# Bases of the decay powers by broadcast transfers, the idle products in one stretch, and the bias as three bf16 products

## The chip, the cores and the metric

The kernel runs on one core of a Trainium2 chip. The metric is the device time of one execution in microseconds; the median of several runs counts. Beside it stands a profiled execution with its trace. The core has five engines that run side by side and wait for each other by semaphores: TensorE (PE, with its weight loads PEld), VectorE (DVE), ScalarE (ACT), GpSimd (POOL) and SyncE (SP), which here only issues transfers. ACT issues a few transfers of its own at the start.

## The reference, cut to what matters

Lightning attention with a decay per head, and a highway layer on its result. There are 4 batches, 8 heads, 768 positions and 64 channels; `lam` is one number per head, and all powers of it are wanted.

```python
Dmask = np.where(rel >= 0, lam[:, None, None] ** rel[None, :, :], 0.0)
lam_pow = lam[:, None, None] ** (pos[None, :, None] + 1)
...
    intra = np.einsum('bhic,bhjc->bhij', qb, kb) * Dmask[None]
    intra = np.einsum('bhij,bhjd->bhid', intra, vb)
    inter = np.einsum('bhid,bhde->bhie', qb * lam_pow[None], kv_state)
    out[:, :, sl] = intra + inter
    kv_state = lam_block[None, :, None, None] * kv_state + np.einsum('bhsd,bhse->bhde', kb_dec, vb)
...
H = np.maximum(x @ w_h, 0.0)
T = 1.0 / (1.0 + np.exp(-(x @ w_t + b_t)))
return (T * H + (1.0 - T) * x).astype(np.float32)
```

Here `x` is the attention's output as 3072 rows of 512, `w_h` and `w_t` are 512 by 512, and `b_t` is a row of 512. Everything is f32 outside; the products on PE are of bf16 numbers, summed in f32.

## The kernel before, in words

The sequence of each batch is cut into three stages of 256 positions, so there are 12 stages, numbered 0 to 11. The decay is put into the operands: q is multiplied by growing powers of lam (`cast_q`, L225 to L235, tile `qb`) and v by falling ones (`cast_v`, L237 to L240, tile `vs`), so that the scores need only a triangular mask. In a stage, k and q are transposed on PE (`trans`, L251, into `bktr` and `bqtr`), copied out of PSUM (`evac_k`, `evac_q`, whose copies go by the helper at L110 for ACT and L112 for DVE and POOL, tiles `kT` and `qT`), multiplied to scores (L279), masked on DVE (L336), and multiplied with v (L358). The state `kv` is summed in PSUM (L284), copied to `ss`, and multiplied with q (L352). The result is copied to `xT` and goes through the two 512 by 512 products of the layer (L388), a sigmoid on ACT, and DVE and POOL work, to the output.

The powers need `lam` on all 128 partitions in two layouts: all eight heads in each row, and for each row the two heads that it holds. Before the change `lam` is brought in as a tile `lam_r` of 4 by 2, and two f32 products (L156, L157) spread it: one with ones and a matrix `lam_d` made on DVE (L152), one with `pick`, a repeated identity (L150). ACT takes the logarithm of the result in PSUM (`ln`, L161), DVE multiplies it with the positions (L163, L168), and ACT takes the exponentials `pow_q8` (L166) and `pow_v` (L171). `cast_q` and `cast_v` of every stage wait for these.

PE does idle products on zeros meanwhile: four at L125, ahead of the two f32 products, and six at L159 behind them; later the plan has spins of the same kind (`spin`, L429).

The bias of the sigmoid is put on all partitions once: `bias` (L426) multiplies a row of ones with `b_r` in f32 into PSUM, DVE copies the result to `b_bc` (token BC), and `begin` (L391) copies `b_bc` into each PSUM tile of the sigmoid's product before that product is added.

The order of the work is written out by hand. What stands before L176 is issued in the order of the program; then come the tokens of PLAN (L17 to L68), one after the other, each issuing its instructions to its engine. Every engine works through its own list in that order. A token is a name, a stage, further indices, `@` and the engine, `=` and PSUM banks. The first ones are a spin (Z.1), the loads and casts of stage 0 (Lv, CV on POOL, Lq, CQ on POOL and DVE), PT, which loads ACT's second activation table, the transposes TQ and TK, their copies EQ and EK, then scores S, states U, the copy KE, masks M; `B=1` is the bias product, and I.0 (L352) follows it on PE. Transfers are issued by SP in the order of the plan, with the two small ones, `lam_r` (L116) and `b_r` (L118), by ACT ahead of everything.

Of the kernel before, what the change touches and what calls it, by code (L numbers as in the profile page):

```python
# [8 lines left out]
F32 = mybir.dt.float32  # L9
BF16 = mybir.dt.bfloat16  # L10
I32 = mybir.dt.int32
AF = mybir.ActivationFunctionType
ALU = mybir.AluOpType
# [1 line left out]


PLAN = """  # L17
Z.1=0 Lv.0.1 CV.0.1@POOL Lq.0.1 CQ.0.1@POOL PT@ACT Lq.0.0 CQ.0.0@DVE TQ.0.2=1 EQ.0.1@ACT Lk.0.0 CK.0.0@DVE TK.0.0=2
Lk.0.1 CK.0.1@POOL EQ.0.0@DVE TK.0.1=3 EK.0.0@ACT EK.0.1@ACT S.0.0=45 Lv.0.0 CV.0.0@DVE U.0.0 KE.0.0@ACT M.0.0.0@DVE
Lq.1.1 S.0.1=60 B=1 M.0.1.0@DVE M.0.1.1@DVE M.0.0.1@DVE BC@DVE I.0=23 U.0.1 KE.0.1@DVE Lq.1.0 CQ.1.2@POOL A.0.0 Lk.1.1  # L20
Lk.1.0 CK.1.2@ACT Lv.1.0 TQ.1.2=4 EQ.1.2@ACT A.0.1 TK.1.2=5 EK.1.2@ACT Z.3=0 D.0.0@ACT Lv.1.1 CV.1.2@DVE SS.1.1=61
# [52 lines left out]
def kernel(  # L74
# [12 lines left out]
    B, H, S, D = q.shape  # L87
    C = 128
    NST = S // (2 * C)
    NP = H // 2  # L90
    DM = H * D
# [6 lines left out]
    singles = ctx.enter_context(tc.tile_pool(name="singles", bufs=1))  # L98
    sb = ctx.enter_context(tc.tile_pool(name="sb", bufs=1))
    ps = ctx.enter_context(tc.tile_pool(name="ps", bufs=1, space=bass.MemoryType.PSUM))  # L100

    V, A, P, T = nc.vector, nc.scalar, nc.gpsimd, nc.tensor
# [5 lines left out]
    def copy(eng, dst, src):  # L108
        if eng == "ACT":
            A.activation(dst, src, AF.Copy)  # L110
        else:
            ENG[eng].tensor_copy(dst, src)  # L112


    lam_r = singles.tile([NP, 2], F32)
    A.dma_start(out=lam_r, in_=lam.rearrange("(h e) -> h e", e=2))  # L116
    b_r = singles.tile([1, DM], F32)
    A.dma_start(out=b_r, in_=moe_b_t.rearrange("(o f) -> o f", o=1))  # L118
    blank = singles.tile([128, 512], BF16)
    V.memset(blank, 0.0)  # L120
    id128 = singles.tile([128, 128], BF16)
    make_identity(nc, id128)
    cold = ps.tile([128, 512], F32, tag="b5", name="cold", bufs=1)
    for _ in range(4):
        T.matmul(cold, lhsT=blank[:, 0:128], rhs=blank, start=True, stop=True)  # L125
    tk_i = singles.tile([128, NST, J], I32)
    P.iota(tk_i, pattern=[[2 * C, NST], [1, J]], base=0, channel_multiplier=J)
# [13 lines left out]
    V.tensor_scalar(row_f, in0=row_i, scalar1=float(Q // NP), scalar2=None, op0=ALU.mult)  # L141
    tq_f = singles.tile([128, NST, Q], F32)
    V.tensor_scalar(tq_f, in0=tq_i, scalar1=row_f, scalar2=None, op0=ALU.add)
    id_f = singles.tile([NP, NP], F32)
    V.tensor_copy(id_f, id128[0:NP, 0:NP])
    A.preload_act_table_set("natural_log_exp_and_others")
    ones = singles.tile([NP, 128], F32)
    V.memset(ones, 1.0)
    pick = singles.tile([NP, 128 // NP, NP], F32)
    V.tensor_copy(pick, id_f[:, None, :].to_broadcast([NP, 128 // NP, NP]))  # L150
    lam_d = singles.tile([NP, NP, 2], F32)
    V.tensor_tensor(lam_d, in0=id_f[:, :, None].to_broadcast([NP, NP, 2]), in1=lam_r[:, None, :].to_broadcast([NP, NP, 2]), op=ALU.mult)  # L152
    kv = ps.tile([128, NP, 128], F32, tag="kv", name="kv", bufs=1)
    V.memset(kv, 0.0)
    lam_ps = ps.tile([128, H + 2], F32, tag="b6", name="lam_ps", bufs=1)
    T.matmul(lam_ps[:, 0:H], lhsT=ones, rhs=lam_d.rearrange("k h e -> k (h e)"), start=True, stop=True, skip_group_check=True)  # L156
    T.matmul(lam_ps[:, H:H + 2], lhsT=pick.rearrange("k p h -> k (p h)"), rhs=lam_r, start=False, stop=True, skip_group_check=True)  # L157
    for _ in range(6):
        T.matmul(cold, lhsT=blank[:, 0:128], rhs=blank, start=True, stop=True)  # L159
    ln = singles.tile([128, H + 2], F32)  # L160
    A.activation(ln, lam_ps, AF.Ln)  # L161
    p_lq = singles.tile([128, NST, 2, Q], F32)
    V.tensor_tensor(p_lq, in0=ln[:, None, H:H + 2, None].to_broadcast([128, NST, 2, Q]),  # L163
                    in1=tq_f[:, :, None, :].to_broadcast([128, NST, 2, Q]), op=ALU.mult)
# [4 lines left out]
                    in1=tk_f[:, :, None, :].to_broadcast([128, NST, H, J]), op=ALU.mult)  # L169
    pow_v = singles.tile([128, NST, H, J], F32)  # L170
    A.activation(pow_v, p_ln, AF.Exp, scale=-1.0)  # L171
    b_bc = singles.tile([128, DM], F32)
    w_f = [singles.tile([128, KC, DM], F32, name=f"w_f{i}") for i in range(2)]
    w_b = [singles.tile([128, KC, DM], BF16, name=f"w_b{i}") for i in range(2)]

# [11 lines left out]
    def bank(key, i, shape, dtype=F32):  # L187
        if key not in made:
            made[key] = ps.tile(shape, dtype, tag=f"b{i}", name=f"b{key[0]}", bufs=1)
        return made[key]  # L190

    def get(*key):
        return made[key]
# [178 lines left out]
    def cols(p):  # L372
        if p > 2:
            return slice(128 * p - 384, 128 * p - 256)
        return slice(0, DM) if p == 2 else slice(256 * p, 256 * p + 256)
# [15 lines left out]
    def begin(n, b, p, eng, bk):  # L391
        z = cols(p)
        copy(eng, bank(("t", n, b, p), bk[0], [C, z.stop - z.start]), b_bc[:, z])
# [23 lines left out]
    def store(n, parts):  # L417
        i = 2 * n * C
        for p in parts:
            nc.sync.dma_start(out=out[i:i + 2 * C].rearrange("(b p) f -> p b f", p=C)[p], in_=get("o_sb", n)[p])  # L420

    def store_part(n, b, p):
        i = (2 * n + b) * C
        nc.sync.dma_start(out=out[i:i + C, cols(p)], in_=get("o_sb", n)[:, b, cols(p)])

    def bias(bk):  # L426
        T.matmul(bank(("bias",), bk[0], [128, DM]), lhsT=ones[0:1], rhs=b_r, start=True, stop=True)  # L427

    def spin(r, bk, idle=[0]):  # L429
        idle[0] += 1  # L430
        t = bank(("spin", idle[0]), bk[0], [128, 512])
        for _ in range(r):
            T.matmul(t, lhsT=id128, rhs=blank, start=True, stop=True)  # L433
# [13 lines left out]
        "TX": lambda a, e, bk: rows(*a, bk), "F": lambda a, e, bk: block(*a, bk), "H": lambda a, e, bk: relu(*a),  # L447
        "G": lambda a, e, bk: sigm(*a), "X": lambda a, e, bk: rest(*a), "Y": lambda a, e, bk: total(*a, e),
        "ST": lambda a, e, bk: store(*a, (slice(0, 119), slice(119, C)) if e else (slice(0, C),)) if len(a) == 1 else store_part(*a),
        "B": lambda a, e, bk: bias(bk), "BC": lambda a, e, bk: copy(e, b_bc, get("bias")), "BP": lambda a, e, bk: begin(*a, e, bk), "Z": lambda a, e, bk: spin(*a, bk),  # L450
        "PT": lambda a, e, bk: A.preload_act_table(AF.Sigmoid),
    }
    in_place = set()
# [3 lines left out]
    for token in PLAN.split():  # L457
        token, _, bk = token.partition("=")
        token, _, eng = token.partition("@")
# [32 lines left out]
```

## Time and profile before

| what | us |
|---|---|
| median of 3 runs (105.47, 106.03, 106.33) | 106.03 |
| profiled execution | 105.67 |
| its span, first to last instruction | 103.6 |
| PE busy in it | 95.2 |
| DVE, ACT, POOL busy | 85.9, 70.1, 71.6 |
| DMA, mean rate over the span | 266 GB/s |

Starts are counted from the first instruction. A profiled execution is longer than its span by what lies before and after it, here 2.07 us. In the busy rows one digit is a fortieth of the span, in tenths; PEclk is the clock that PE was granted. In the chain of waits every piece is what the next one waited for, or what stood before it on the same engine. The timeline gives start, duration, engine, line, and the tile written and the tiles read; in square brackets stands the idle time before and what ended it.

### The profile page before, as it was taken

To read this page: it belongs to the slowest core of one execution; us is meant where nothing else is said; L and a number is where in the kernel's file an instruction comes from. 1 tells how busy PE (TensorE), PEld (TensorE's weight loads), DVE (VectorE), ACT (ScalarE), POOL (GpSimd) and SP (SyncE) were. 2 spreads that over 40 slices of the span, in tenths; PEclk is the share of its full clock that TensorE was granted. 3 is DMA by queue.
4 is the path that set the end of the run, shared out by engine and by line. 5 is a ranking of instruction groups with operands and counts; after the bars stand their busy time and mean duration, and the time that the engine had idled before them with its cause. 6 is when DMAs were issued, how large, how long until landed. Compare 5 with 4: busy or idle time off the path is not lost.

```text
span 103.6 us, 3953 instructions
## 1 busy us (share of the span) xinstructions
PE 95.2 (92%) x1667; PEld 61.0 (59%) x1687; DVE 85.9 (83%) x148; ACT 70.1 (68%) x113; POOL 71.6 (69%) x64
## 2 busy tenths in 40 slices
PE   5976998999999999999999999999999999999940
PEld 1524475576547666577767665668666767555630
DVE  4475863779599979999999999998997988899980
ACT  3446327959738879786599879997684786475410
POOL 6192702655979999999995059799899974255450
PEclk9999557999999999999999999999999999999997
DMA  1999999999999999999999999998310491047564
GB/s 35 311 302 341 293 362 355 384 328 331 285 326 311 307 309 320 292 342 272 286 317 325 376 360 344 367 313 278 136 75 0 168 384 69 0 166 274 216 224 139
DMA packets 33483, 27.52 MB, mean 266 GB/s; under 512 B 1465, under 2 KB 26425, under 8 KB 33466
## 3 DMA queue, kind: packets, MB, share of 16 engines
q1 hardware_dynamic: 33456, 27.27, 84.3%
q8 instruction: 13, 0.21, 0.8%
q14 instruction: 4, 0.03, 0.2%
q10 hardware_dynamic: 10, 0.00, 0.0%
HBM read 20.97 MB, written 6.29 MB: 263 GB/s over the span
## 4 chain that ended last, share of the span: by engine, by line
PE 86%; DVE 4%; POOL 2%; ACT 2%; issue 2%; DVEq 0%; POOLq 0%
PE bh L388 20%; PE bt L388 19%; PE bs L279 9%; PE bo L358 7%; PE bqtr L251 6%; PE bx L382 6%; PE bktr L251 5%; PE bo L352 5%; PE kv L284 3%; PE bbias L427 2%; PE cold L125 2%; POOL qb L233 1%; POOL vs L239 1%; ACT kT L110 1%; PE bspin L433 1%
## 5 line engine op out<-in xcount | busy, mean ns | idle before, releaser
L336 DVE TENSOR_TENSOR m<-bs,tri 128x512 bf16<-128x512 f32 x48 | 31.0, 683 | 2.5 <-PE bs L279 2.0
L415 POOL TENSOR_TENSOR ob<-y,w 128x512 f32<-128x512 bf16 (+1 forms) x20 | 22.2, 1119 | 14.9 <-DVE y L402 9.6
L388 PEld LDWEIGHTS <-xT 128*128 128x128 bf16 x208 | 18.0, 98 | 16.0 <-issue 0.2
L388 PE MATMUL bh<-w_b,xT 128*128 128x512 bf16 (+2 forms) x95 | 23.2, 361 | 0.5
L388 PE MATMUL bt<-w_b,xT 128*128 128x512 bf16 (+2 forms) x94 | 23.2, 361 | 0.5 <-issue 0.2
L239 POOL TENSOR_TENSOR vs<-vf,pow_v 128x1024 bf16<-128x1024 f32 (+1 forms) x11 | 21.0, 1912 | 3.4 <-ACT pow_v L171 2.2
L397 ACT ACTIVATE g<-bt 128x512 f32<-128x512 f32 (+2 forms) x26 | 14.5, 565 | 10.2 <-PE bt L388 7.3
L233 POOL TENSOR_TENSOR qb<-qf,pow_q 128x1024 bf16<-128x1024 f32 (+1 forms) x10 | 18.6, 1858 | 1.7 <-DMA qf<-in_q_dram 1.7
L408 DVE SCALAR_TENSOR_TENSOR w<-g,bx 128x512 bf16<-128x512 f32 (+2 forms) x26 | 16.0, 639 | 1.3 <-ACT g L397 1.0
L110 ACT ACTIVATE qT<-bqtr 128x1024 bf16<-128x1024 bf16 (+1 forms) x12 | 11.9, 989 | 5.6 <-PE bqtr L251 5.6
L110 ACT ACTIVATE xT<-bo 128x512 bf16<-128x512 f32 x22 | 12.6, 597 | 4.1 <-PE bo L358 4.0
L279 PE MATMUL bs<-qT,kT 64*64 64x128 bf16 x384 | 14.7, 222 | 0.6 <-ACT kT L110 0.5
L402 DVE SCALAR_TENSOR_TENSOR y<-bh,g 128x512 bf16<-128x512 f32 (+1 forms) x20 | 13.1, 665 | 1.5 <-PE bh L388 1.3
L279 PEld LDWEIGHTS <-kT 64*64 64x64 bf16 x384 | 11.3, 108 | 5.0 <-issue 2.5
L110 ACT ACTIVATE ss<-kv 128x512 bf16<-128x512 f32 x15 | 9.0, 597 | 4.1 <-PE bs L279 3.3
L110 ACT ACTIVATE bt<-b_bc 128x512 f32<-128x512 f32 (+1 forms) x18 | 10.4, 586 | 0.3
L284 PE MATMUL kv<-vs,kb 64*64 64x64 bf16 x320 | 9.8, 201 | 0.3 <-DVE vs L239 0.2
L358 PE MATMUL bo<-m,vs 64*64 64x128 bf16 x384 | 8.5, 226 | 0.0
L251 PE MATMUL bktr<-id,kb 128*128 128x128 bf16 x96 | 7.9, 226 | 0.7 <-POOL kb L112 0.7
L284 PEld LDWEIGHTS <-kb 64*64 64x64 bf16 x320 | 8.0, 111 | 0.8 <-issue 0.8
L251 PE MATMUL bqtr<-id,qb 128*128 128x128 bf16 x96 | 7.8, 227 | 0.6 <-POOL qb L233 0.6
L358 PEld LDWEIGHTS <-vs 64*64 64x64 bf16 x384 | 6.3, 110 | 2.9 <-issue 2.3
(63 smaller groups left out, 111.2 us busy)
## 6 DMA issues: line engine op xcount, KB each, us to landing
vf<-in_v_dram SPq DMA_DIRECT2D x24, 256.0 KB, 5.9
qf<-in_q_dram SPq DMA_DIRECT2D x24, 256.0 KB, 5.5
kf<-in_k_dram SPq DMA_DIRECT2D x24, 256.0 KB, 5.4
out_dram<-ob SPq DMA_DIRECT2D x11, 512.0 KB, 3.9
w_f<-in_moe_w_t_dram SPq DMA_DIRECT2D x2, 512.0 KB, 5.9
w_f<-in_moe_w_h_dram SPq DMA_DIRECT2D x2, 512.0 KB, 8.3
out_dram<-ob SPq DMA_DIRECT2D x1, 256.0 KB
out_dram<-ob SPq DMA_DIRECT2D x2, 64.0 KB, 1.8
```

Source lines behind the costliest of these rows:

```text
L110: A.activation(dst, src, AF.Copy)
L233: ENG[eng].tensor_tensor(new(("qb", n), [128, Q, 2, D])[:, :, es].rearrange("p j e d -> p e j d"), in0=get("qf", n)[:, es].rearrange("p e ...
L239: ENG[eng].tensor_tensor(new(("vs", n), [128, H, J, D])[:, heads(p)], in0=get("vf", n)[:, heads(p)].rearrange("p h (j d) -> p h j d", j=J) ...
L251: T.transpose(t[:, i], turned(x, n, c), id128)
L279: T.matmul(get("s", n, e, hp // 2)[half(b), hp % 2, j, :], lhsT=get("kT", n)[half(e), hp, j, half(b)], rhs=get("qT", n)[half(e), hp, b * C ...
L284: T.matmul(kv[half(e), hp, half(e)], lhsT=get("kb", n)[half(b), j, 2 * hp + e, :], rhs=get("vs", n)[half(b), 2 * hp + e, j, :], start=firs ...
L336: V.tensor_tensor(new(("m", n, e, u), [128, 2, J, C]), in0=get("s", n, e, u), in1=tri[:, None].to_broadcast([128, 2, J, C]), op=ALU.mult)
L358: T.matmul(get("o", n, b)[half(e), hp, :], lhsT=get("vs", n)[half(b), 2 * hp + e, j, :], rhs=get("m", n, e, hp // 2)[half(b), hp % 2, j, : ...
L388: T.matmul(t, lhsT=get("xT", n)[:, j, b * C:(b + 1) * C], rhs=w_b[w][:, j, z], start=(j == 0 and not w), stop=(j == KC - 1), skip_group_ch ...
L397: A.activation(new(("g", n, b), [C, DM], F32)[:, z], get("t", n, b, p), AF.Sigmoid)
L408: V.scalar_tensor_tensor(new(("w", n, b), [C, DM])[:, z], in0=get("g", n, b)[:, z], scalar=1.0, in1=x.rearrange("p j f -> p (j f)")[:, z], ...
L415: ENG[eng].tensor_tensor(o, in0=y, in1=get("w", n, b)[:, z], op=ALU.subtract)
```

## The change

The bases come as two transfers onto 128 partitions, into one tile `lam_b`, in place of the two f32 products and what made their operands. All fourteen idle products stand ahead; the six behind the f32 products are gone with these. The bias is split into three bf16 terms that sum to it: b_s[0] is the bias rounded, b_d the rest, b_s[1] that rounded, b_s[2] what is then left. Four tokens BS.0 to BS.3 do this at the very head of the plan, on ACT, DVE, ACT and DVE; the bias product becomes three bf16 products added in PSUM.

```diff
 PLAN = """
-Z.1=0 Lv.0.1 CV.0.1@POOL Lq.0.1 CQ.0.1@POOL PT@ACT Lq.0.0 CQ.0.0@DVE TQ.0.2=1 ...
+BS.0@ACT BS.1 BS.2@ACT BS.3 Z.1=0 Lv.0.1 CV.0.1@POOL Lq.0.1 CQ.0.1@POOL PT@ACT Lq.0.0 CQ.0.0@DVE TQ.0.2=1 ...
...
-    lam_r = singles.tile([NP, 2], F32)
-    A.dma_start(out=lam_r, in_=lam.rearrange("(h e) -> h e", e=2))
+    lam_b = singles.tile([128, H + 2], F32)
+    A.dma_start(out=lam_b[:, 0:H], in_=lam.rearrange("(o h) -> o h", o=1).to_broadcast([128, H]))
+    A.dma_start(out=lam_b[:, H:H + 2], in_=lam.rearrange("(o h e) -> o h e", o=1, e=2).to_broadcast([128 // NP, NP, 2]))
     b_r = singles.tile([1, DM], F32)
     A.dma_start(out=b_r, in_=moe_b_t.rearrange("(o f) -> o f", o=1))
...
-    for _ in range(4):
+    for _ in range(14):
         T.matmul(cold, lhsT=blank[:, 0:128], rhs=blank, start=True, stop=True)
...
-    id_f = singles.tile([NP, NP], F32)
-    V.tensor_copy(id_f, id128[0:NP, 0:NP])
     A.preload_act_table_set("natural_log_exp_and_others")
-    ones = singles.tile([NP, 128], F32)
-    V.memset(ones, 1.0)
-    pick = singles.tile([NP, 128 // NP, NP], F32)
-    V.tensor_copy(pick, id_f[:, None, :].to_broadcast([NP, 128 // NP, NP]))
-    lam_d = singles.tile([NP, NP, 2], F32)
-    V.tensor_tensor(lam_d, in0=id_f[:, :, None].to_broadcast([NP, NP, 2]), in1=lam_r[:, None, :].to_broadcast([NP, NP, 2]), op=ALU.mult)
     kv = ps.tile([128, NP, 128], F32, tag="kv", name="kv", bufs=1)
     V.memset(kv, 0.0)
-    lam_ps = ps.tile([128, H + 2], F32, tag="b6", name="lam_ps", bufs=1)
-    T.matmul(lam_ps[:, 0:H], lhsT=ones, rhs=lam_d.rearrange("k h e -> k (h e)"), start=True, stop=True, skip_group_check=True)
-    T.matmul(lam_ps[:, H:H + 2], lhsT=pick.rearrange("k p h -> k (p h)"), rhs=lam_r, start=False, stop=True, skip_group_check=True)
-    for _ in range(6):
-        T.matmul(cold, lhsT=blank[:, 0:128], rhs=blank, start=True, stop=True)
     ln = singles.tile([128, H + 2], F32)
-    A.activation(ln, lam_ps, AF.Ln)
+    A.activation(ln, lam_b, AF.Ln)
...
+    b_s = singles.tile([1, 3, DM], BF16)
+    b_d = singles.tile([1, DM], F32)
+    one_b = singles.tile([1, 128], BF16)
+    P.memset(one_b, 1.0)
...
+    def split(i, eng):
+        if i == 0:
+            copy(eng, b_s[:, 0], b_r)
+        elif i == 1:
+            V.tensor_tensor(b_d, in0=b_r, in1=b_s[:, 0], op=ALU.subtract)
+        elif i == 2:
+            copy(eng, b_s[:, 1], b_d)
+        else:
+            V.tensor_tensor(b_s[:, 2], in0=b_d, in1=b_s[:, 1], op=ALU.subtract)
+
     def bias(bk):
-        T.matmul(bank(("bias",), bk[0], [128, DM]), lhsT=ones[0:1], rhs=b_r, start=True, stop=True)
+        t = bank(("bias",), bk[0], [128, DM])
+        for i in range(3):
+            T.matmul(t, lhsT=one_b, rhs=b_s[:, i], start=(i == 0), stop=(i == 2))
```

On the engines' lists this stands as follows. ACT issues three transfers (`lam_b` twice, then `b_r`), loads its first table, does ln and the two exponentials, then BS.0 and BS.2, then the second table load. DVE does the two products behind ln, then BS.1 and BS.3, then its half of `qb`. PE does fourteen idle products and the spin, then the transposes. SP's list is as before. POOL writes `one_b` ahead of its first `vs`.

## Prediction

> **What bounds the kernel now.** I read the busy slices first, then the chain of waits of the first 22 us in order of time, then the timeline of 0 to 14 us for what stands behind each step, then the stages for the clock and the DMA rings by stretch for when the small transfers land.
>
> ```profile
> PE   5976998999999999999999999999999999999940
> PEclk9999557999999999999999999999999999999997
> ```
>
> A digit is 2.6 us. (The first 9s of the clock are no measure: the idle products there step by 0.43 us, twice the 0.216 of full rate.) From about 17 us to 100 us PE is the bound: no wait of PE longer than 0.5 us is left there. So what PE gains or loses before 17 us should reach the end nearly whole. The change touches only what lies before 13.4 us.
>
> ```profile
> 4.12 0.19 ACT ln L161
> 4.57 0.24 ACT pow_q L166
> 4.81 0.14 ACT pow_v L171
> 5.09 1.04 POOL vs L239
> 6.13 1.46 POOL qb L233
> 7.63 0.63 PE bqtr L251 x8
> 8.29 0.60 ACT qT L110
> 8.92 0.69 DVE qT L112
> 9.61 0.61 DVE vs L239
> 10.26 0.53 PE kv L284 x12
> 10.90 0.43 PE bs L279 x14
> 11.32 2.00 PE bbias L427 x2
> 13.32 0.54 PE bo L352 x4
> ```
>
> These are the two places that count. The powers come from ln at 4.12, through POOL's products, to the first transposes (bqtr) at 7.63; and the f32 bias product holds PE for 2.00 us, from 11.32 to 13.32. What it holds back, bo of L352, needs ss, which ACT had at 11.53 (10.93 and 0.60), so all of the bias is on the path.
>
> ```profile
> 1.25 1.89 PE L125 MATMUL cold<-blank 128*128 128x512 bf16 x4 [1.25 <-DVE blank L120]
> 2.86 0.15 DVE L152 TENSOR_TENSOR lam_d<-id_f,lam_r 4x8 f32<-4x8 f32 x1
> 4.97 1.28 ACT L451 ACT_TABLE_LOAD   x1
> 5.88 0.80 DVE L233 TENSOR_TENSOR qb<-qf,pow_q 128x512 bf16<-128x512 f32 x1 [1.23 <-DMA qf<-in_q_dram]
> 8.29 0.60 ACT L110 ACTIVATE qT<-bqtr 128x512 bf16<-128x512 bf16 x1 [2.04 <-PE bqtr L251]
> ```
>
> Here DVE makes its half of qb at 5.88 to 6.68, 0.95 us before the transposes; ACT has nothing to do from 6.25 (4.97 and 1.28) to 8.29. That is all the slack into which the four new steps (BS.0 to BS.3) are put.
>
> **The change part by part.** The profiled execution took 105.67 us, of which 103.6 are the span; the median of the three runs is 106.03, so 0.36 is added to what comes out for the profiled one.
>
> *Bias.* Removed: 2.00 us of PE. Added: three bf16 products of 512 columns. The granted clock is 0.5 from 10.2 to 17.0 us. A product of that size at the low rate is the idle one: six of them step by 0.43 (the weight loads before them start at 4.41, 4.84, 5.27, 5.69, 6.12). Three cost 1.28, so the path gets 0.72 shorter. At the full clock (four bh products in 0.86 us, 0.216 each) they would cost 0.65; that end belongs to a rival.
>
> *Bases of the powers.* Removed from PE: the two f32 products (0.52 and 0.43 on the chain); from DVE: id_f, ones, pick and lam_d (0.15, 0.17, 0.37, 0.15), all ahead of ln. ln then waits for two transfers of 128 rows (32 and 8 bytes a row), ACT's first and second issue, with b_r third. Issues cost ACT 0.55 for lam_r and 0.23 for b_r, and SP 0.64 for 128 rows of qf (1.27 for two). With 0.55 for each of the new ones, from 0.80, the first table load starts near 2.2 instead of 1.64 and ends near 3.5 (1.28): ln is not sooner than that. When does the second transfer land? Nothing in this trace is it, so from both sides. The low end is lam_r: issued at 0.80, used at 2.86 without a wait, thus 2.06 at most; from 1.38 that gives 3.45. The high end is qf, also 128 rows: 3.5 from issue to landing in the first 2 us, so 4.9. The nearest is b_r, which was issued at that very place, 1.38:
>
> ```profile
> q10 hardware_dynamic: 8, 0.00, 0.2%
> ...
> q10 hardware_dynamic: 1, 0.00, 1.3%
> ...
> q10 hardware_dynamic: 1, 0.00, 0.1%
> ```
>
> The ring of ACT moved lam_r's eight packets before 2.0 us, one packet of b_r between 2.6 and 3.0, and its last between 3.0 and 3.5. SP's ring moved 417 packets between 2 and 3 us, so 128 rows want 0.3 us more: I take 3.8. ln then starts at 3.8 instead of 4.12, and pow_v, 0.83 after the start of ln as before (4.12 to 4.95), is done at 4.63.
>
> *The split of the bias, BS.0 to BS.3.* It stands ahead of the whole plan, so on ACT it is queued before the second table load and the copy of qT, and on DVE before qb. It alternates between the two: ACT, DVE, ACT, DVE, each waiting for the other. They work on one row of 512, but the time of the rows goes by the length of a row: ACT's 512 copies take 0.60 (xT; 0.64 from SBUF, w_b), DVE's products of 512 take 0.68 alone (vs) and 0.80 beside POOL's qb, which is running here; I take 0.74. With 0.03 for each hand-over (ln ends 4.30, p_lq starts 4.33): 0.60 + 0.03 + 0.74 + 0.03 + 0.60 + 0.03 + 0.74 = 2.77, from 4.63 to 7.40. Only then does DVE come to qb, which its data would have let it do at 5.88: 0.68, to 8.08, and 0.05 to PE. The transposes start at 8.13 instead of 7.63: **0.50 later**. POOL, which was last, is done with its half by about 7.3 (vs and qb start 0.32 sooner) and no longer matters. The table load follows BS.2 (6.63) and ends at 7.91, before qT at 8.8: hidden, with 0.9 to spare. From bqtr to kv every step of the chain hands on to the next with 0.02 to 0.05 us, so 0.50 reaches kv; the kf that held up kb on POOL (landed at 8.47) comes in that shade.
>
> *Idle products.* Fourteen at 0.43 are 6.0 us: 1.25 to 7.25 instead of 6.75, the spin after them to 7.7. PE waits for qb until 8.13, so they cost nothing; if qb came at 7.6 the spin would just reach it.
>
> *Rest.* one_b on POOL: its 64x256 selections end at 2.85 and it waits for pow_v until 5.09, so free. kv's memset on DVE moves up by 0.9 us into idle time. SP's list is the same.
>
> **Sum:** 0.50 later at kv, 0.72 saved at the bias: 0.22 sooner at bo. Downstream follow work that ACT and PE do back to back (transposes of the second stage, kT at 17.31), and its data wait for PE and not the reverse: qb of that stage is on hand at 12.69 and used at 14.85. So 105.67 - 0.22 = 105.45 for the profiled execution, 106.03 - 0.22 = **105.8 us** for the median. Bounds: with ln at 3.5 and the short durations (0.60, 0.68) qb is ready 0.08 later than before, in all 0.64 sooner, 105.4; with 4.9 and the long ones (0.64, 0.80) bqtr starts 1.92 later, in all 1.2 later, 107.2.
>
> **Rivals.**
>
> *The small transfers come late (slower).* Same place, ln's wait. At the landing of qf, 4.9, with my middle durations: pow_v 5.73, BS.3 8.50, bqtr 9.23, 1.60 later; less 0.72: 0.88, **106.9 us**. It decides from a landing at 4.02 on, where the loss equals 0.72. For it: b_r, with a single row, did not move until 2.6 although it was issued by 1.61. Against: the rows here carry 40 bytes, not 2 KB. The Trainium skill, page "DMA: Bandwidth & Descriptors", section "Issuing engines are not separate DMA queues", says that transfers issued by ACT and by SP run on the same 16 engines and interleave; by that rule the late landing and 106.9 are what to expect, by lam_r's row 105.4, and b_r's packets are on the rule's side.
>
> *The clock rises one stretch sooner (faster by more).* PE was busy 3.34 of 3.40 us between 10.2 and 13.6 and the clock stayed at 0.5; after 13.6 to 17.0 it rose. The first stretch differs by 2 us of one-row f32 products. If bf16 products count there and the f32 ones did not, the rise comes at 13.6. The work of 13.86 to 17.29 on the chain then goes at nearly double rate (8 transposes in 0.45 instead of 0.97, 32 bo in 0.57 against 16 in about that): some 1.5 us less, with 0.22 a total of 1.7, **104.3 us**. Against it: the new products have one row too. The Trainium skill, page "TensorE: Matmul & The Clock Gate", section "What's actually happening", has the full clock follow a busy window of 3.4 us that runs free of the kernel; the steps at 10.2 and 17.0 are two such windows apart, which agrees, but what counts as busy this trace can't say.
>
> *The loads are pushed back.* 256 rows more at 417 a us are 0.6 us for every load behind them. kb on POOL is then done at 9.7 instead of 9.08, and the scores start some 0.6 later instead of 0.5: in all 0.1 sooner, **105.9 us**, no change.
>
> **How the numbers follow.** Forecast 0.60, late transfers 0.22, clock 0.12, loads 0.06. A difference of 1% (1.06 us) is about what a measurement of this kernel tells from none. The forecast and the pushed loads lie within it; the clock is beyond it, faster, nearly always; late transfers reach over 107.1 only with the long durations, about half the time: faster 0.12, same 0.76, slower 0.12. The range 104.9 to 107.0 leaves out most of the clock and the top of the late transfers. The likeliest's own range is 105.3 to 106.4.
>
> **What would show it.** Right: DVE goes from BS.3 straight to qb near 7.4, without a wait for qf; bqtr near 8.1; the bias about 1.3 us on PE; bo of L352 (now L344) near 13.1. Wrong: ln after 4.2 (late transfers); a PEclk back at 9 by 14 us (clock); a DVE qb still at 5.9, which would mean that the order of the queue is not what holds it; a PE wait for DMA or POOL between 17 and 30 us that takes back what was won.

## The result, and the profile after

The changed kernel takes 111.5 us (median of 4 runs, 110.13 to 111.85), against 105.75 for the kernel before beside it. The ratio is 1.050, with a 95% interval of 1.037 to 1.064: slower by 5%, where 105.8 us and no change had been forecast. The profiled execution took 110.13 us with a span of 108.2, 4.6 more than the span before. One thing is needed to read single times: executions of one and the same kernel differ by 2 us and more (13 of the kernel before in one batch: 104.1 to 107.5), so every ratio compares the faster executions of the two kernels.

The busy slices of the page after, 2.7 us to a digit:

```profile
PE   5930679989999999999999999999999999999950
PEclk9999655599999999999999999999999999999997
```

PE now has a hole in the third to fifth slice, and the clock's 5s come later. From the ninth slice on the rows look as before: all of the loss is made in the first 22 us. The chain of waits there, in order of time (start, duration, what):

```profile
1.28 5.64 DMA lam_b<-in_lam_dram
...
7.01 0.22 ACT ln L149
7.24 0.02 issue
7.26 0.22 DVE p_lq L151
7.48 0.02 issue
7.50 0.24 ACT pow_q L154
7.74 0.13 ACT pow_v L159
7.88 0.53 ACT b_s L110
8.40 0.02 issue
8.43 1.19 DVE b_d L422
9.61 0.02 issue
9.63 0.64 ACT b_s L110
10.27 0.02 issue
10.30 0.75 DVE b_s L426
11.05 0.61 DVE qb L225
11.66 0.14 issue
11.80 1.02 PE bqtr L243 x8
...
15.02 0.53 PE kv L276 x9
...
16.08 1.39 PE bbias L431 x3
17.47 0.54 PE bo L344 x4
```

Read it against the chain before, station by station:

| from, to | before | after | more |
|---|---|---|---|
| start to the end of pow_v | 4.95 | 7.88 | 2.93 |
| to the first transposes (bqtr 7.63, 11.80) | 2.68 | 3.92 | 1.24 |
| to the bias (11.32, 16.08) | 3.69 | 4.28 | 0.59 |
| the bias itself | 2.00 | 1.39 | -0.61 |
| sum, at bo (13.32, 17.47) | | | 4.15 |
| bo to the end of the span | 90.3 | 90.7 | 0.4 |

The first row is the largest: a transfer of 128 rows of 8 bytes was issued at 1.28 and ln could not start before 7.01. The 0.59 of the third row are the transposes, now at half rate (1.02 instead of 0.63), and DVE's vs (0.81 instead of 0.61). The stages show two more things (columns: stretch and its length, then the busy time of PE, PEld, DVE, ACT and POOL, the granted clock, the DMA share and GB/s):

```profile
2.60:6.80 4.20, 3.70 (x13) 1.26 (x11) 0.44 (x1) 1.28 (x1) 0.46 (x2) 1.00 0.51 151
6.80:10.20 3.40, 0.00 (x0) 0.00 (x0) 1.50 (x3) 1.67 (x5) 2.18 (x2) 1.00 1.13 333
10.20:13.60 3.40, 1.80 (x16) 1.62 (x16) 1.82 (x4) 2.10 (x4) 3.35 (x3) 0.68 1.13 317
13.60:17.00 3.40, 2.68 (x52) 1.67 (x51) 3.40 (x6) 2.12 (x4) 0.82 (x1) 0.50 1.13 323
17.00:20.40 3.40, 3.40 (x62) 2.34 (x60) 2.85 (x4) 0.63 (x2) 1.38 (x2) 0.50 1.07 361
```

While the small rows go, the transfers move 151 GB/s, where they moved 296 before. PE, without work from about 6.3 to 11.8, then works at half rate up to about 21.7: some 10.2 us of it, where it was 6.8.

### The profile page after: what moved, and what is told of

The parts are those of the page before. It is cut to its first block, busy times and chain, and to the rows that moved or that the text cites. A ratio compares the mean times of both kernels' runs of the same rounds, so it can differ in the third digit from the quotient of the medians.

```text
span 108.2 us, 3958 instructions
## 1 busy us (share of the span) xinstructions
PE 95.1 (88%) x1668; PEld 61.3 (57%) x1688; DVE 86.9 (80%) x146; ACT 71.2 (66%) x115; POOL 74.9 (69%) x65
## 4 chain that ended last, share of the span: by engine, by line
PE 76%; DVE 9%; DMA 5%; ACT 3%; issue 3%; ACTq 0%; DVEq 0%
PE bh L380 19%; PE bt L380 18%; PE bs L271 8%; PE bo L350 7%; PE bqtr L243 6%; PE bktr L243 5%; DMA lam_b<-in_lam_dram 5%; PE bx L374 5%; PE bo L344 4%; PE kv L276 3%; DVE m L328 2%; PE bbias L431 1%; DVE b_d L422 1%; ACT b_s L110 1%; DVE vs L231 1%
## 5 line engine op out<-in xcount | busy, mean ns | idle before, releaser
L407 POOL TENSOR_TENSOR ob<-y,w 128x512 f32<-128x512 bf16 (+1 forms) x20 | 22.3, 1121 | 16.8 <-DVE y L394 11.8
L389 ACT ACTIVATE g<-bt 128x512 f32<-128x512 f32 (+2 forms) x26 | 14.5, 565 | 10.3 <-PE bt L380 7.0
L225 POOL TENSOR_TENSOR qb<-qf,pow_q 128x1024 bf16<-128x1024 f32 (+1 forms) x10 | 19.6, 1962 | 0.1
L243 PEld LDWEIGHTS <-qb 128*128 128x128 bf16 x96 | 6.4, 105 | 7.6 <-issue 6.0
```

The costliest lines, as they stand in the source:

```text
L225: ENG[eng].tensor_tensor(new(("qb", n), [128, Q, 2, D])[:, :, es].rearrange("p j e d -> p e j d"), in0=get("qf", n)[:, es].rearrange("p e ...
L243: T.transpose(t[:, i], turned(x, n, c), id128)
L389: A.activation(new(("g", n, b), [C, DM], F32)[:, z], get("t", n, b, p), AF.Sigmoid)
L407: ENG[eng].tensor_tensor(o, in0=y, in1=get("w", n, b)[:, z], op=ALU.subtract)
```

## The experiments

The theory after the result, A: the landing of the second small transfer delays ln by 2.9 us; the split, standing ahead of DVE's qb, adds 1.2; the bias gives 0.6 back. The rivals: B, the split costs most; and for the landing three causes, A1 small rows, A2 the same few bytes read by all rows, A3 any rows of ACT among SP's loads. A2 is called "one address" in the expectations. To be exact, the second transfer reads four pairs of numbers of lam, 32 bytes in all, each pair for 32 rows; the first reads these 32 bytes for each of its 128 rows. Later came C (DVE and POOL stop each other), with D (a late load) as its rival, and E (the clock), with F (PE waits for other engines and loads anyway). Times of one batch are compared with the kernel before in that batch; batches ran on different chips, so two changed kernels are compared by their ratios or their traces.

### Each half alone

Bases by transfers and the fourteen products, with the bias left in f32:

```diff
-BS.0@ACT BS.1 BS.2@ACT BS.3 Z.1=0
+Z.1=0
...
-            T.matmul(t, lhsT=one_b, rhs=b_s[:, i], start=(i == 0), stop=(i == 2))
+        T.matmul(bank(("bias",), bk[0], [128, DM]), lhsT=one_f, rhs=b_r, start=True, stop=True)
```

> Bases by the two transfers and the fourteen idle products, the bias still one f32 product and no split. Theory A (the landing of the second small transfer costs about 2.9 us at ln, the split the rest): ln near 7.0, bqtr 2.7 after the end of pow_v, so near 10.6, the bias 2.0 on PE; 109 us, 3 over before. Rival B (the alternating split at the head of the queues costs most): ln near 7.0 matters little, time within 1 us of before.

Measured: ln at 6.68, bqtr at 10.23, 110.54 us (four executions, 108.11 to 111.91) against 105.99. A stands, and B, which wanted the time within 1 us of before, does not; by the median 1.5 us more were lost than A had worked out. DVE's vs took 2.39 us here instead of 0.68, and the clock was at half until 24.2.

The other half, f32 bases with the split at the head of the plan and three bf16 products:

> Bases by f32 products as before, the bias split at the head of the plan and three bf16 products. Theory A: ln at 4.1 as before, bqtr 0.9 to 1.2 later than 7.63, the bias 0.6 shorter: 105.9 to 106.4 us, no change that 1% shows. Rival B: 109 us or more.

Measured: 108.6 us. ln at 4.12 and bqtr at 8.87, 1.24 later, as A has it; but the whole lost 2.6 by the median, where A had said 0.2 to 0.7. The four executions lie between 106.37 and 109.05, so the size is not settled. The profiled one took 109.05; in its trace bo, behind the bias, starts 2.1 us later than before and the end comes 3.7 later. The timeline between 10.3 and 13.2 us shows one thing beside the wait:

```profile
10.46 1.90 POOL L237 TENSOR_TENSOR qb<-qf,pow_q 128x1024 bf16<-128x1024 f32 x1 [0.93 <-DMA qf<-in_q_dram]
10.75 2.15 DVE L243 TENSOR_TENSOR vs<-vf,pow_v 128x512 bf16<-128x512 f32 x1
12.96 0.47 PE L288 MATMUL kv<-vs,kb 64*64 64x64 bf16 x10 [1.43 <-DVE vs L243]
```

Before, DVE's vs ran at 9.53, ahead of POOL's qb at 10.79, in 0.68 us. Pushed back by 1.2, it falls right behind the start of POOL's 1.9 us and ends 0.54 after POOL does. Theory C: the two do not share, one waits until the other's instruction is over. The same is seen in the changed kernel at the split:

```profile
8.02 1.04 POOL L231 TENSOR_TENSOR vs<-vf,pow_v 128x512 bf16<-128x512 f32 x1 [4.90 <-ACT pow_v L159]
8.43 1.18 DVE L422 TENSOR_TENSOR b_d<-b_r,b_s 1x512 f32<-1x512 f32 x1 [0.84 <-ACT b_s L110]
9.02 1.49 POOL L225 TENSOR_TENSOR qb<-qf,pow_q 128x512 bf16<-128x512 f32 x1
```

DVE's b_d ends 0.55 after POOL's vs (9.06), and POOL's qb 0.9 after b_d (9.61), its length when alone being half of the 1.9 that 1024 take. A row of a single partition blocks as 128 do.

The trace before already had it: beside POOL's qb DVE's cast of k took 1.16 us (6.71 to 7.87), and 0.43 in a run where POOL stood idle. It is not all that the split alone lost in its trace: half rate lasted 10.2 us there too, and a later DVE product, of 1024 columns at 26.04, took 2.18 beside POOL's vs, where one of its size at 17.24 took 1.22.

The test of C, on the split alone: POOL reads one column of DVE's vs before its next qb.

```diff
-CQ.1.2@POOL
+HOLD CQ.1.2@POOL
...
+        "HOLD": lambda a, e, bk: P.tensor_copy(hold, get("vs", 0)[:, 0, 0, 0:1]),
```

> The run with the split alone, and POOL, before its product for stage 1 (qb, 1.9 us), reads one column of what DVE's vs of stage 0 has written, so that the two no longer run at once. Theory C (DVE's product with two SBUF operands stands still while POOL works; it took 2.15 us beside POOL's qb and 0.68 alone): DVE's vs takes 0.7, kv starts near 11.5 instead of 13.0, 1.4 us under the run with the split alone, near 107.2. Rival D (vs waited for its load): DVE's vs still ends near 12.8, and POOL's wait makes it slower by about 1 us.

```profile
11.16 0.68 DVE L244 TENSOR_TENSOR vs<-vf,pow_v 128x512 bf16<-128x512 f32 x1
...
12.05 1.90 POOL L238 TENSOR_TENSOR qb<-qf,pow_q 128x1024 bf16<-128x1024 f32 x1
```

vs takes 0.68 again, though PE was at half rate in this execution, and the time is 106.6 us, a ratio of 1.013 (1.002 to 1.023) to before. C is shown for the instruction; what it is worth in time is not, since the split alone had an execution of 106.37 as well. D, a late load, falls: with POOL out of the way vs begins and ends at once. The Trainium skill, page "SBUF — State Buffer", section "Terms", says that DVE and GpSimd arbitrate for one pair of ports, exclusively and for a whole instruction, and that the loser blocks; the 1.18 and 2.15 us agree.

### The split in other places

BS.0 ahead of the second table load, BS.1 behind DVE's first cast of k, BS.2 between the copies of kT, BS.3 on POOL. First with f32 bases:

```diff
-PT@ACT ... CK.0.0@DVE TK.0.0=2 ... EK.0.0@ACT EK.0.1@ACT
+BS.0@ACT PT@ACT ... CK.0.0@DVE BS.1@DVE TK.0.0=2 ... EK.0.0@ACT BS.2@ACT BS.3@POOL EK.0.1@ACT
```

> As the run with the split alone, but its four steps stand where ACT, DVE and POOL had idle time before: BS.0 ahead of the second table load, BS.1 behind DVE's first cast of k, BS.2 between the two copies of kT, BS.3 on POOL. Both theories: bqtr at 7.6 as before; the bias takes 1.3 to 1.4 instead of 2.0, so 105.1 us, 0.6 under before, if what the bias gives reaches the end; 105.7 if something else holds bo back.

Measured: 105.24 against 105.99, ratio 0.998 (0.989 to 1.007): no change that can be claimed. In the profiled execution, 103.87 us, bqtr starts at 7.84 and bo already at 11.80, 1.5 us sooner than in the trace before, and its span is 1.5 shorter too, 102.1. This execution kept the full clock after 7.8 us. Its lead had been greater between, 2.1 at the second transposes of k; the chain says where the rest went:

```profile
10.77 6.19 DMA w_f<-in_moe_w_t_dram
16.97 0.05 issue
17.02 0.61 POOL w_b L112
...
19.09 0.81 PE bt L392 x3
```

PE, that early, waits for the weights of the layer, whose transfer starts at 10.77. So what is saved before 17 us reaches the end only as far as the loads allow.

Then the same places in the changed kernel:

> The changed kernel with the four steps of the split in those later places. Theory A: ln near 7.0, bqtr near 10.6 instead of 11.8; 1.2 us under the changed kernel, about 110 us, still 4 over before. Rival B: back to about 106 us.

Measured: 108.74 us, ratio 1.039 (1.027 to 1.050), bqtr at 11.16 with ln as late as 7.61. From ln to bqtr are 3.55 us instead of 4.79, the 1.2 worked out. Against the changed kernel's 1.050 that is some 1.2% less, though the intervals overlap; B falls, as a loss of 2.7 to 5.0% stays.

### Why the small transfer is slow

Three probes: the kernel before, with one transfer that nothing uses in the place of the second base transfer.

```diff
+    probe = singles.tile([128, 2], F32)
+    A.dma_start(out=probe, in_=lam.rearrange("(o h e) -> o h e", o=1, e=2).to_broadcast([128 // NP, NP, 2]))
```

> The kernel before, and one transfer more that nothing uses, in the place of the second base transfer (ACT's second issue): 128 rows of 8 bytes, all from the address of lam. Theory A1 (rows under 512 bytes are slow to write, wherever they are read): its rows are spread over 2 us or more, and the loads behind it move at half rate meanwhile, so that DVE gets its half of qf 1 to 2 us after 5.9. Theory A2 (only reads of one and the same address are slow): the same here, but not with distinct addresses. Theory A3 (any 128 rows that ACT issues share the engines with SP's loads row by row): the same here and with 512 bytes a row.

The same with `in_=q[0, 0, 0:128, 0:2]`:

> As the run with 128 rows of 8 bytes from one address, but each row from an address of its own, 256 bytes apart (the first two numbers of 128 rows of q). A1: as slow as with one address, over 2 us from first to last row. A2: done within 0.6 us, the loads hardly later. A3: as slow.

And with 128 numbers a row, from `q[0, 0, 0:256, :]`:

> As these, but 128 rows of 512 bytes, each from its own address (64 KB in all). A1 and A2: done within 0.6 us of its first row, the loads 0.2 us later, for the 64 KB. A3: over 2 us.

Packets of ACT's ring (count, MB, share of 16 engines), all rows from the same 32 bytes, 3.4 to 6.2 us (there were none between 2.8 and 3.4):

```profile
q10 hardware_dynamic: 146, 0.00, 2.8%
```

Distinct addresses of 8 bytes, 2.8 to 3.4 us, then 3.4 to 6.2:

```profile
q10 hardware_dynamic: 144, 0.00, 13.5%
...
q10 hardware_dynamic: 2, 0.00, 0.2%
```

512 bytes a row, the same two stretches:

```profile
q10 hardware_dynamic: 108, 0.05, 28.7%
...
q10 hardware_dynamic: 38, 0.02, 2.1%
```

From the same 32 bytes the packets are spread over more than 2 us (first at 3.9, last at 6.0 by the trace), and all transfers together moved 248 GB/s between 2.6 and 6.8 us, against 291 in the probe with distinct addresses. Distinct ones of the same size are nearly all through before 3.4. Rows of 512 bytes are between 3.1 and 3.6. So neither the size of the rows (A1) nor their number (A3) is it, but the many reads of the same bytes (A2). The distinct addresses lie in q and not in lam; that lam itself is slow to read is unlikely, as the four rows of lam_r, read from it, are through before 2.0, but repeated reads of another tensor were not tried. What these probes do not show is a loss at DVE: it got its qf at 6.77 with the same 32 bytes and at 6.74 with 512 bytes a row, but at 6.82 in a kernel without any probe (the split in later places), so that is no measure.

The same in the changed kernel itself, both transfers from distinct addresses:

```diff
-    A.dma_start(out=lam_b[:, 0:H], in_=lam.rearrange("(o h) -> o h", o=1).to_broadcast([128, H]))
-    A.dma_start(out=lam_b[:, H:H + 2], in_=lam.rearrange("(o h e) -> o h e", o=1, e=2).to_broadcast([128 // NP, NP, 2]))
+    A.dma_start(out=lam_b[:, 0:H], in_=q[0, 0, 0:128, 0:H])
+    A.dma_start(out=lam_b[:, H:H + 2], in_=q[0, 0, 0:128, 0:2])
...
-    A.activation(ln, lam_b, AF.Ln)
+    A.activation(ln, lam_b, AF.Copy, scale=0.02)
```

> The changed kernel, but the two transfers onto 128 partitions read a different address for every row (rows of q, in place of lam; a scaled copy stands for the logarithm, so the powers are other numbers of the same size). Theory A2 (many rows read from one address are what is slow): both transfers are done by 4, ln starts near 4, 3 us sooner than in the changed kernel, and bqtr near 8.8; 108 to 109 us, as with the split alone. A1 or A3 (small rows, or rows of ACT among SP's loads): ln stays near 7 and the time at 111.

```profile
3.98 0.21 ACT L149 ACTIVATE ln<-lam_b 128x10 f32<-128x10 f32 x1 [0.21 <-DMA lam_b<-in_q_dram]
```

ln at 3.98 instead of 7.01, by the addresses alone, and 300 GB/s moved between 2.6 and 6.8 us instead of 151; bqtr at 8.76; 108.95 us, ratio 1.037 (1.012 to 1.062). Of the 3.0 us gained at ln 2.4 are left at bo and 1.5 at the end of the trace. What is lost still is about what the split alone lost.

Both causes away, distinct addresses and the later places:

> The changed kernel with both causes taken away: transfers from distinct addresses (rows of q, a scaled copy for the logarithm, so other powers) and the split in its later places. If the two causes are the whole: ln near 4.0, bqtr near 7.7, 105 to 105.8 us, as the f32 bases with the late split (105.2). If something else in the change costs (the fourteen products, the order of the loads): 107 or more.

Measured: ln at 4.00, bqtr at 7.74, the bias in 0.75 on PE; 104.27 us, ratio 0.980 (0.970 to 0.991). The two causes are the whole loss; without them the change would even be 1 to 3% faster than before. Their costs do not add up: each taken away by itself brought 1.050 down only to 1.039 and 1.037, and half rate lasted 10.2 us in both traces; with both gone the clock stayed full from 7.1 us on. This kernel is only a measure: its bases are not those of lam. The fourteen idle products cost nothing here (their end at 7.3, the spin's at 7.6).

### The clock

The changed kernel with 34 idle products:

> The changed kernel with 34 idle products instead of fourteen, so that PE works until about 11 us, when its transposes can start. Theory E (part of the loss is the clock: PE stands idle for 5.5 us and then works at half rate for 10.2 us, where before it was 6.8): the granted clock stays full for longer or all the time, 1.5 to 2.5 us under the changed kernel, 109 to 110 us. Rival F (the work of those 10 us waits for DVE, ACT and loads anyway): within 0.5 us of the changed kernel.

Measured: 110.61 us (four executions, 108.87 to 111.92), against 106.24 before. The half-rate stretch moved to 14.6 to 21.4 us and is 6.8 long, as before the change, and yet this profiled execution ends 4.8 us later than the one before. For E that is inconclusive, and it speaks against the clock as the main part. With 38, and more in the later waits:

```diff
-    for _ in range(14):
+    for _ in range(38):
...
-TK.0.1=3 EK.0.0@ACT EK.0.1@ACT S.0.0=45
+TK.0.1=3 Z.4=0 EK.0.0@ACT EK.0.1@ACT S.0.0=45 Z.2=0
```

> The changed kernel with 38 idle products at the start, four behind the transposes of k and two behind the first scores, so that PE hardly stands idle before 15 us. Theory E: no half-rate stretch after the first rise; the bias in 0.8 instead of 1.4 us; 108 to 109 us, 2.5 to 3.5 under the changed kernel, and what stays over the kernel before with spins (105.0) is the wait for ln and the split, 3.5 to 4. Rival F: the same clock or not, 110.5 to 112 us.

The stretch of 11.4 to 21.7 us of the changed kernel:

```profile
11.40:21.70 10.30, 9.19 (x136) 6.61 (x137) 7.07 (x11) 4.45 (x8) 5.65 (x5) 0.50 1.11 339
```

And of this one:

```profile
11.40:21.70 10.30, 8.83 (x180) 5.27 (x179) 8.53 (x14) 6.79 (x11) 5.57 (x5) 1.00 1.07 334
```

Measured: 107.72 us (10 runs, 107.33 to 107.85), ratio 1.011 (1.008 to 1.015) to before, although ln came at 7.45 and bqtr at 12.23, later than in the changed kernel. Six spins and 24 more idle products give back about 4 us (1.0504 to 1.011, each against before in its own batch): PE issues 180 products where it issued 136 (ten of the 44 more are idle ones), and ACT and DVE follow. So half rate costs this kernel time, as E has it, and F falls. The Trainium skill, page "TensorE: Matmul & The Clock Gate", section "What's actually happening", lets the clock fall after an idle window of 3.4 us and counts the windows free of the kernel; the hole of 5.5 us, and half rate for 10.2 (three times 3.4), agree. The kernel before does not agree: its clock fell at 10.2 after a stretch in which PE was at work for more than half of the time.

```profile
6.80:10.20 3.40, 1.92 (x33) 1.27 (x33) 2.34 (x4) 1.68 (x3) 1.39 (x2) 1.00 1.10 345
```

In other traces it fell as well after a stretch of 3.4 us with 2.31 of work (the probe with distinct addresses), and stayed full after 2.39 (the split in later places) and 2.24 (both causes away). So no idle window is needed, and busy time alone does not say when it falls.

Spins in the kernel before, six of them, and in the one with the split in later places:

```diff
-Z.1=0 Lv.0.1 ... Lk.0.1 CK.0.1@POOL ... S.0.0=45
+Z.3=0 Lv.0.1 ... Z.3=0 Lk.0.1 CK.0.1@POOL ... S.0.0=45 Z.1=0
```

> The kernel before with only those six idle products more. Theory E: 104.8 us, about 1 under before; F: 105.9 to 106.8.

> f32 bases, the split in its later places, and idle products put where PE waits in the first 10 us: two more before the first transposes, three between the two halves of the transposes of k, one behind the first scores. Theory E: the clock is up in more of the executions, 104.3 us, 1.5 under before. F: 105.2, as without them; or slower by the products themselves, at most 0.9 us at half rate.

Measured: 104.97 and 104.16 us against 106.24, but with ratios of 1.003 (0.994 to 1.012) and 1.002 (0.997 to 1.006): no gain over the kernel before is shown by the comparison. With the split in later places and the full clock kept, PE waits for the weights again, here until 19.20.

These runs also size the clock's part in the loss. The profiled executions with spins have spans of 105.6 us (changed) and 102.8 (before), 2.8 apart; without spins they are 4.6 apart. By these four single executions, an estimate, some 1.8 us of the loss come through the clock and 2.8 by the waits themselves.

## Why the prediction was wrong

**The step that failed** is the landing of the second small transfer: "I take 3.8", with 4.9 as the upper end. ln started at 7.01, and pow_v, forecast to end at 4.63, ended at 7.88: 3.25 of the 4.8 us between the forecast span and the measured one. The rows chosen to bound it (lam_r's four, b_r's one, qf's 128) each read an address of their own; none read the same 32 bytes 128 times, and that is what costs, as the probes showed. The rival of late transfers had the place and the sign right, and a price of 106.9 that could not be high enough, since its end was one of those rows.

**The clock as a fixed stretch.** The sum priced PE's work at the rate that each microsecond had before. But the stretch hangs on what PE does: idle for 5.5 us, it then had half rate for 10.2 us instead of 6.8. That was in no term; the one rival on the clock looked only the other way. What it cost the change is known only roughly: the table shows 0.4 in the transposes and at most 0.4 behind bo, the spins give some 1.8. Neither is to be added to the table's 4.15 and 0.4, which hold it already.

**The split, 2.77.** By its own chain, from 7.88 to 11.05, it took 3.17. The four steps one after the other and qb right behind them, without a wait for qf, came as said. Mis-sized was DVE's first step, 1.19 instead of 0.74: it does not run slower beside POOL, it waits for POOL's instruction to end. The 0.80 of DVE's qb, from which the term was averaged, was itself such a wait: it ended 0.55 after POOL's vs. The split alone made bqtr 1.24 later instead of 0.50.

**"From bqtr to kv every step of the chain hands on to the next": wrong.** It holds if nothing else moves. In the changed kernel this stretch grew by 0.59. In the split alone DVE's vs came behind POOL's qb and lost 1.5 us more. A chain that is shifted meets other neighbours.

**The bias.** 1.28 was forecast at half rate, 1.39 measured; 0.61 was saved instead of 0.72. At the full clock it takes 0.75 (11.05 to bo at 11.80 with the split in later places).

**That gains before 17 us reach the end.** For a loss this held: 4.15 at bo, 4.6 at the end. For a gain it held in part: with the split in later places the lead was 1.5 at bo, 2.1 at the second transposes of k and 1.5 at the end, as the weights were late next.

**Idle products.** They cost nothing, as said; they ended sooner than forecast (near 5.9), since the clock rose at 4.6 in that execution.

## What to carry to other kernels

Before replacing a small product by a broadcast transfer, ask how many rows read the same bytes: here 128 rows of 8 bytes out of the same 32 took over 2 us, and from 128 addresses 0.2 to 0.4. When a step early in a kernel is moved, look up what DVE and POOL do side by side at the new place, and how much work is left to PE in each few microseconds; here the first cost 1.5 us on one product and the second, by estimate, 1.8. When several causes are found, take them away together as well: here each alone gave back a little over 1%, and both 7%. And bound an unknown cost by a row that does the same thing to the memory, not just one of the same shape.

## What the runs showed of the hardware that was not expected

- 128 rows of 8 bytes read out of the same 32 bytes of HBM: first packet at 3.9, last at 6.0; from distinct addresses 3.0 to 3.3. In the changed kernel the transfers moved 151 GB/s between 2.6 and 6.8 us, and 300 with distinct addresses. Where in the path of a read this is lost stays open.
- DVE with two operands in SBUF stands still for the whole of a POOL instruction and the reverse, with one partition as with 128 (1.18 us for b_d, which took 0.67 where POOL stood idle). DVE's cast of k, with one operand, was held too (1.16 instead of 0.43). DVE's masks, with one operand in PSUM, ran beside POOL's qb in the kernel before at 0.62 each.
- The granted clock fell after a stretch of 3.4 us in which PE was busy for 1.92 (the kernel before), and stayed at half through one with 3.34 of work. No trace here shows what it counts.
- A granted clock of 1.0 ahead of its first record is no measure: the split with POOL waiting shows a mean of 0.999, while its first record is at 19.5 us and its transposes before that took 1.01 us, against 0.61 at full rate.
